# A recurrence and a gated product on one core: v loaded in fp32 by SP and cast by GpSimd, w_in issued together and earlier, some loads held back

## The chip, the cores and the metric

The kernel runs on one core of a Trainium2 chip. The metric is the time of one execution on the device in microseconds (us), less is better. Engines are named as in the profile: PE is TensorE (PEld its weight loads), DVE is VectorE, ACT is ScalarE, POOL is GpSimd, SP is SyncE.

## What is computed

```python
def _attn_ref(q, k, v, f_logit):                 # each (4, 8, 768, 48)
    f = 1.0 / (1.0 + np.exp(-f_logit))
    state = np.zeros((B, H, D, D))
    for t in range(S):
        state = f[:, :, t, :, None] * state + np.einsum('bhd,bhe->bhde', k[:, :, t], v[:, :, t])
        y[:, :, t] = np.einsum('bhd,bhde->bhe', q[:, :, t], state)

def _moe_ref(x, w_in, w_out, a, b):              # x (3072, 384), w_in (384, 2048), w_out (2048, 384)
    h = x @ w_in
    P = a[0] + a[1] * h + a[2] * h * h + a[3] * h * h * h
    Q = 1.0 + np.abs(b[0]) * np.abs(h) + np.abs(b[1]) * h * h
    return (P / (Q + 1e-06)) @ w_out
```

A gated linear recurrence over 768 steps is run for 4 batches of 8 heads of size 48; its output, with the heads side by side, goes through a matrix product, a rational function of each element and a second matrix product. All inputs and the output are fp32.

## The kernel before, in words

The sequence is cut into chunks of 256 steps. A *unit* is one chunk of one batch, so there are 12 units (unit n is chunk n // 4 of batch n % 4). Within a unit the recurrence is done in blocks of 64 steps as matrix products, and the state is handed on from block to block and from chunk to chunk.

The order of all work is written out by hand in the string `ORDER`: each entry is a step with the number of its unit, and each engine and each queue carries out its own steps in the order in which they stand there. The steps of one unit n:

- `ld n f|k|q|v` loads an input. f, k and q come in fp32 by SP's queue; v comes by POOL's queue, which casts it to bf16 on the way (tile `vn`). The tiles of the loads have three buffers each.
- `ef`, `ls` (ACT) make the logarithm of the gate, `cs` (PE) its running sum, `A` (ACT) the exponentials, `xa` (DVE) the products of k (x=1) and q (x=0) with them, `T` (PE) and `Te` (ACT, DVE in unit 0) their transposes.
- `sc` (PE) are the scores of a half of the heads, `mk` (DVE) multiplies them with the causal mask out of PSUM.
- `yi` (PE) is the part of the output from the old state, `yb` (PE) the part from inside the block. `yb` uses v as its weights in pieces of 32 columns, since a head has 48; the piece that lies across two heads comes from the tile `vmp`, which `vm n 0` and `vm n 1` (POOL) fill with 16 columns each.
- `kv` (PE) multiplies k with v into the state, `si` adds the old state, `ae` (ACT) and `st` (DVE) scale it; `ye` (ACT, in part DVE in unit 0) brings the output to SBUF as `xT`.
- `h n m0 m1` (PE) multiplies `xT` with four blocks of `w_in` (`ha`, `hb` do the same in two parts); `hy` copies the result, `sq`, `ab`, `p1`, `p2`, `pm`, `tv`, `gm` (DVE), `u` (PE), `ln`, `lz`, `ex` (ACT) make the rational function, and `zd`, `ta` are additions done by DMAs on POOL's queue.
- `o` (PE) multiplies with `w_out`, `oe` copies, `so` stores.
- `wi m0 m1` and `wo m0 m1` load four blocks of `w_in` and `w_out` by POOL's queue with a cast to bf16; `dz` are products that nobody reads.

A step with `>mark` waits until the step of that name has ended (`behind`); what stands behind it on the same engine or queue waits with it. In the order before, `wi 8 12` stands behind unit 0's first `kv`, `wi 12 16 >ls.1` waits for unit 1's logarithm, and `wi 4 8` and `wi 0 4` follow on POOL's queue among the copies and loads of v.

Of the kernel before, what the change touches and what calls it, by code (L numbers as in the profile page):

```python
# [38 lines left out]
hy 2 8 12; wo 0 4; mk 3 0; cs 4 @0; ls 5; vm 4 0; h 2 12 16 @2; vm 3 0; tv 0 0 8; A 4 0; ld 8 f; ld 5 q; A 4 1
xa 4 0; yi 3 1 @3; ld 6 k; yb 3 0 2; hy 2 4 8; ld 6 q; u 1 4 8 @0; xa 4 1; hy 2 12 16; yb 3 2 4; gm 0 8 16  # L40
cs 5 @1; ld 6 v; ye 3 s; T 4 @2; gm 0 0 8; A 5 0; ln 1 4 8; h 3 0 4 @3; p1 2 0 16; Te 4 s; h 3 12 16 @0
ab 2 0 16; hy 3 0 4; o 0 1 8 12 @2; tv 1 0 8; A 5 1; kv 4 @3; hy 3 12 16; sq 2 0 16; u 1 0 4 @1; ae 4; ex 1 8 16
o 0 0 8 12; si 4 0; o 0 1 12 16; xa 5 1; vm 5 1; ln 1 0 4; h 3 8 12 @0; zd 2 8 16; p2 2 0 16; ld 8 k; ef 6
h 3 4 8 @1; ef 7; pm 2 0 16; hy 3 8 12; o 0 1 4 8; hy 3 4 8; sc 4 1 @0; o 0 1 0 4; ls 6; mk 4 1; ta 2 8 16
sc 4 0 @1; ex 1 0 8; o 0 0 0 4; ld 9 f; xa 5 0; cs 6 @0; mk 4 0; o 0 0 4 8; A 6 1; o 0 0 12 16; st 4 0; A 6 0
yb 4 0 2 @1; ab 3 0 16; yb 4 2 4; oe 0 0 2 s; yi 4 0; yi 4 1; si 4 1; sq 3 0 16; ye 4 s; T 5 @2; ef 8
u 2 0 4 @1; Te 5 s; h 4 4 8 @0; st 4 1; zd 3 8 16; ln 2 0 4; gm 1 8 16; h 4 12 16 @2; lz 2 8 16; p1 3 0 16
sc 5 0 @3; h 4 0 4 @1; xa 6 0; hy 4 4 8; vm 6 1; ta 2 0 8; gm 1 0 8; hy 4 12 16; ld 9 q; h 4 8 12 @0; vm 5 0
ld 7 k; ld 7 v; hy 4 0 4; mk 5 0; vm 6 0; u 2 4 8 @2; zd 3 0 8; hy 4 8 12; pm 3 0 16; o 1 1 4 8 @1; ln 2 4 8
o 1 0 0 4; ex 2 8 16; sc 5 1 @2; kv 5 @0; mk 5 1; yi 5 0 @3; yb 5 0 2; ls 7; o 1 0 12 16; sq 4 0 16; o 1 0 4 8  # L50
# [575 lines left out]
```

## Time and profile before

| | |
|---|---|
| timed runs | 215.76, 216.56, 216.99 us; median 216.56 us |
| profiled execution | span 214.4 us from the first to the last instruction; no other time of its own is given |
| busy us in the span | PE 201.0, DVE 201.7, ACT 195.8, POOL 83.7 |
| granted TensorE clock | 1.000 |
| DMA | 43.20 MB, mean 202 GB/s |
| POOL's DMA queue (q0) | 23.86 MB, 21,520 packets |
| SP's DMA queue (q1) | 18.68 MB, 39,360 packets |

In rows of instructions the first number is the start and the second the duration in us, then engine, line of the kernel, operation, the tile written, the tile read, shape and count; a bracket names the idle time before it and what ended that. In rows of groups the numbers behind the bars are busy us, mean ns of one, and idle us before them.

### The profile page before, as it was taken

The numbers are of one execution on the slowest core, as the hardware profiler recorded it, in microseconds if no ns is written. First come the engines' busy times: TensorE is split into PE (matmuls) and PEld (weight loads), VectorE is DVE, ScalarE is ACT, GpSimd is POOL, SyncE is SP. The second block draws the span as 40 slices with busy tenths as digits, with TensorE's granted clock in tenths as the row PEclk, the third lists the DMA queues.
The fourth block names the chain that finished last, engine by engine and source line by source line (L and its number), as shares of the span: only waits on it lengthen the run. The fifth ranks groups of instructions, "written<-read, shape, count | busy, mean of one in ns | idle before, by whom it ended". The sixth has DMA issues, their size and how long they took to land.

```text
span 214.4 us, 7128 instructions
## 1 busy us (share of the span) xinstructions
PE 201.0 (94%) x3166; PEld 139.9 (65%) x3166; DVE 201.7 (94%) x213; ACT 195.8 (91%) x204; POOL 83.7 (39%) x93
## 2 busy tenths in 40 slices
PE   5875999899999999999999899999999999999993
PEld 1544587567767686586687587686577676776461
DVE  4786899999999999999999999999999999999991
ACT  3574689999999999999999999999999999999990
POOL 5161009009165072183270496696350603114200
PEclk9999999999999999999999999999999999999999
DMA  5999999999999999999999499999499896988823
GB/s 143 240 257 217 201 242 197 195 223 223 187 200 248 247 235 219 253 228 203 192 292 193 81 294 215 209 225 208 89 192 200 164 196 126 174 282 151 187 84 148
DMA packets 61199, 43.20 MB, mean 202 GB/s; under 512 B 51184, under 2 KB 55024, under 8 KB 61168
## 3 DMA queue, kind: packets, MB, share of 16 engines
q0 software_dynamic: 21520, 23.86, 67.3%
q1 hardware_dynamic: 39360, 18.68, 34.5%
q8 instruction: 25, 0.41, 0.8%
q10 hardware_dynamic: 288, 0.20, 0.3%
q14 instruction: 6, 0.05, 0.1%
HBM read 25.17 MB, written 4.72 MB: 139 GB/s over the span
## 4 chain that ended last, share of the span: by engine, by line
PE 39%; DVE 29%; ACT 14%; DMA 9%; issue 6%; SPq 2%; POOL 1%; DVEq 0%
PE hp L454 13%; PE op L567 12%; DVE gall L557 6%; DMA w_in_sb<-in_moe_w_in_dram 6%; DVE gall L545 4%; ACT qi L527 4%; ACT hy L484 4%; DVE z L497 3%; DVE h L489 3%; DVE scm L353 3%; DMA fn<-in_f_logit_dram 3%; PE u L505 3%; DVE gall L531 3%; PE y L367 2%; DVE hy L536 2%
## 5 line engine op out<-in xcount | busy, mean ns | idle before, releaser
L567 PE MATMUL op<-w_out_sb,gall 128*128 128x384 bf16 x384 | 69.2, 326 | 0.4 <-DVE gall L557 0.4
L454 PE MATMUL hp<-xT,w_in_sb 128*128 128x256 bf16 x564 | 66.7, 273 | 2.1 <-DMA w_in_sb<-in_moe_w_in_dram 2.0
L454 PEld LDWEIGHTS <-w_in_sb 128*128 128x128 bf16 x564 | 54.2, 98 | 11.5 <-DMA w_in_sb<-in_moe_w_in_dram 2.5
L567 PEld LDWEIGHTS <-gall 128*128 128x128 bf16 x384 | 36.1, 98 | 23.6 <-DVE gall L557 0.8
L484 ACT CAST hy<-hp 128x1024 bf16<-128x1024 f32 x47 | 48.1, 1076 | 2.3 <-PE hp L478 1.4
L527 ACT ACTIVATE qi<-lq 128x2048 bf16<-128x2048 f32 (+1 forms) x26 | 48.0, 1861 | 0.1
L360 POOL COPY vmp<-vn 128x128 bf16<-128x128 bf16 x24 | 35.2, 1516 | 28.4 <-DMA vn<-in_v_dram 22.7
L549 POOL DMA_DIRECT2D gall<-hy x20 | 20.0, 1068 | 53.9 <-ACT lsp L276 10.6
L523 ACT ACTIVATE lq<-z 128x2048 f32<-128x2048 bf16 (+1 forms) x20 | 36.8, 1874 | 0.0
L353 DVE TENSOR_TENSOR scm<-sc,mask 128x1024 bf16<-128x1024 f32 x24 | 29.0, 1215 | 1.9 <-PE sc L345 1.7
L489 DVE TENSOR_TENSOR h<-hy 128x4096 bf16<-128x4096 bf16 (+2 forms) x19 | 28.5, 1500 | 0.0
L557 DVE TENSOR_TENSOR gall<-gall,qi 128x4096 bf16<-128x4096 bf16 (+2 forms) x17 | 28.2, 1666 | 0.2
L545 DVE TENSOR_TENSOR gall<-gall,h 128x4096 bf16<-128x4096 bf16 (+2 forms) x17 | 28.1, 1652 | 0.0
L519 POOL DMA_DIRECT2D z<-h x17 | 19.3, 1366 | 17.0 <-PE u L505 6.0
L302 ACT ACTIVATE A<-cs 128x768 f32<-128x768 f32 (+1 forms) x26 | 19.4, 799 | 1.8 <-PE cs L286 1.8
L193 POOL DMA_DIRECT2D vn<-in_v_dram x12 | 12.4, 1030 | 15.7 <-PE y L367 7.9
L531 DVE TENSOR_SCALAR gall<-hy,a_sb 128x4096 bf16<-128x4096 bf16 (+1 forms) x14 | 16.9, 1208 | 0.0
L536 DVE TENSOR_SCALAR hy<-hy,a_sb 128x4096 bf16<-128x4096 bf16 (+1 forms) x14 | 16.6, 1185 | 0.0
L497 DVE TENSOR_SCALAR z<-hy 128x4096 uint16<-128x4096 uint16 (+2 forms) x19 | 15.7, 834 | 0.4 <-ACT hy L484 0.4
L330 ACT COPY qkT<-tp 128x1024 f32<-128x1024 f32 x11 | 11.6, 1058 | 3.2 <-PE tp L320 3.2
L320 PE MATMUL tp<-ident,qkp 128*128 128x128 bf16 x192 | 12.9, 219 | 0.8 <-DVE qkp L308 0.5
L320 PEld LDWEIGHTS <-qkp 128*128 128x128 bf16 x192 | 11.5, 98 | 2.5 <-DVE qkp L308 0.9
(73 smaller groups left out, 255.8 us busy)
## 6 DMA issues: line engine op xcount, KB each, us to landing
gall<-hy POOLq DMA_DIRECT2D x18, 512.0 KB, 7.1
z<-h POOLq DMA_DIRECT2D x15, 512.0 KB, 8.4
fn<-in_f_logit_dram SPq DMA_DIRECT2D x11, 384.0 KB, 8.5
kn<-in_k_dram SPq DMA_DIRECT2D x11, 384.0 KB, 12.1
qn<-in_q_dram SPq DMA_DIRECT2D x11, 384.0 KB, 11.3
out_dram<-osb SPq DMA_DIRECT2D x11, 384.0 KB, 5.1
vn<-in_v_dram POOLq DMA_DIRECT2D x12, 192.0 KB, 8.9
w_in_sb<-in_moe_w_in_dram POOLq DMA_DIRECT2D x4, 384.0 KB, 10.1
```

What stands on the lines that cost most here:

```text
L320: nc.tensor.transpose(t[:, x, i, p, :], s["qk"][:, i, x, 2 * p:2 * p + 2, :].rearrange("t h d -> t (h d)"), ident)
L353: return nc.vector.tensor_mul(t, s["sc", g].rearrange("s r a i t -> s (r a) (i t)"), mb)
L360: nc.gpsimd.tensor_copy(s["vm"][:, :, :, 32 * x:32 * x + 16], src)
L454: nc.tensor.matmul(t[:, m - m0, :], w_in_sb[:, kk, m * P:(m + 1) * P], s["x"][:, kk].rearrange("p i j t -> p (i j t)"), start=(kk == 0), s ...
L484: (nc.scalar.copy if eng == "s" else nc.vector.tensor_copy)(fl(big(s, "hy", "hy", 3), m0, m1), fl(s["hp", m0], 0, m1 - m0))
L489: return nc.vector.tensor_mul(fl(big(s, "h2", "h2", 2), m0, m1), fl(s["hy"], m0, m1), fl(s["hy"], m0, m1))
L523: nc.scalar.activation(fl(lq, m0, m1), fl(s["z"], m0, m1), AF.Ln, scale=regs[2], bias=1.0 + 1e-6)
L527: nc.scalar.activation(fl(qi, m0, m1), fl(lq, m0, m1), AF.Exp, scale=-1.0)
L531: return nc.vector.tensor_scalar(fl(big(s, "g", "gall", 3), m0, m1), fl(s["hy"], m0, m1), a_sb[:, 3:4], a_sb[:, 2:3], op0=ALU.mult, op1=AL ...
L545: return nc.vector.tensor_mul(fl(s["g"], m0, m1), fl(s["g"], m0, m1), fl(s["h2"], m0, m1))
L557: return nc.vector.tensor_mul(fl(s["g"], m0, m1), fl(s["g"], m0, m1), fl(qi, m0, m1))
L567: nc.tensor.matmul(s["op", j][:, j, 0:DM], s["g"][:, m, P * j:P * j + P], w_out_sb[:, m, :], start=(s["on", j] == 1), stop=(s["on", j] == KF))
```

## The change

v is loaded in fp32 by SP's queue into a tile with a single buffer. A new step `vc n par` casts the heads of one parity into `vpd`, where each head has 64 columns: even heads lie at columns 0 to 47 and odd ones at 16 to 63, the rest is zero. `yb` and `kv` read their weights and operand from there, and `vm` and `vmp` are gone. `vc` runs on POOL, but for unit 0 (one on ACT, one on DVE) and unit 10 (both on DVE). Many `vc` steps have a mark, and `ld n+1 v` stands behind the second `vc` of unit n. Because SP's queue issues in order, a v load that waits for its buffer holds the loads behind it.

The four loads of `w_in` are issued one after the other behind `ls.0.2.4`, unit 0's second logarithm. `ld 2 k` waits for `xa.1.0`, and `ld 2 q`, `ld 3 f`, `ld 3 k`, `ld 3 q` stand behind it. The mask is bf16. All else stands in the order as before.

The start of the order, before and after:

```
-ld 0 q 0 2; ld 1 f; ld 0 v; ab_ a s; ld 1 k; fa; ld 1 q; ef 0 2 4; ef 0 0 2; cz 3; ls 0 0 2; ls 0 2 4; cz 1
-cs 0 2 4 @2; cs 0 0 2 @3; A 0 0 2 4; dz 4 @0; A 0 1 2 4; xa 0 0 2 4; A 0 1 0 2; xa 0 1 2 4; A 0 0 0 2
-xa 0 1 0 2; T 0 2 4 @0; vm 0 1; kv 0 @3; Te 0 2 4; wi 8 12; xa 0 0 0 2; ae 0; sc 0 1 @0; si 0 0; mk 0 1
-T 0 0 2 @2; ef 1; dz 5 @1; fr; Te 0 0 2; ld 2 f >mk.0.1; ls 1; ld 3 f; st 0 0; sc 0 0 @0; ld 2 k; cs 1 @2
-wi 12 16 >ls.1; mk 0 0; ld 2 q; ld 3 k; yi 0 1 @1; vm 0 0; A 1 1; ld 1 v; ld 3 q; yb 0 2 4; yb 0 0 2; A 1 0
-si 0 1; wi 4 8; ye 0 0 1 v; ye 0 1 3 s; xa 1 1; wi 0 4; h 0 8 12 @1; xa 1 0; ld 2 v; fb; T 1 @0; hy 0 8 12 v
+ld 0 q 0 2; ld 0 v; ld 1 f; ab_ a s; ld 1 k; fa; ld 1 q; ef 0 2 4; ef 0 0 2; cz 3; ls 0 0 2; ls 0 2 4
+wi 8 12 >ls.0.2.4; wi 12 16; wi 4 8; wi 0 4; cz 1; cs 0 2 4 @2; cs 0 0 2 @3; A 0 0 2 4; dz 4 @0; A 0 1 2 4
+xa 0 0 2 4; A 0 1 0 2; xa 0 1 2 4; A 0 0 0 2; xa 0 1 0 2; T 0 2 4 @0; vc 0 0 s; vc 0 1 v; ld 1 v; kv 0 @3
+Te 0 2 4; xa 0 0 0 2; ae 0; sc 0 1 @0; si 0 0; mk 0 1; T 0 0 2 @2; ef 1; dz 5 @1; fr; Te 0 0 2; ld 2 f >mk.0.1
+ls 1; st 0 0; sc 0 0 @0; cs 1 @2; mk 0 0; yi 0 1 @1; A 1 1; yb 0 2 4; yb 0 0 2; A 1 0; si 0 1; ye 0 0 1 v
+ye 0 1 3 s; xa 1 1; h 0 8 12 @1; xa 1 0; ld 2 k >xa.1.0; ld 2 q; ld 3 f; ld 3 k; ld 3 q; fb; T 1 @0; hy 0 8 12 v
```

The steps of v in the rest of the order after: `vc 1 0 >ab.0.8.12`, `vc 1 1 >sq.0.8.12; ld 2 v`; `vc 2 0; vc 2 1; ld 3 v` behind `sc 2 0`; `vc 3 0 >p2.0.0.8`, `vc 3 1 >st.2.0; ld 4 v`; `vc 4 0 >pm.1.0.8`, `vc 4 1 >mk.3.1; ld 5 v`; and so on to `vc 9 0; vc 9 1; ld 10 v`, `vc 10 0 v; vc 10 1 v; ld 11 v`, `vc 11 0 >p1.8.0.16`, `vc 11 1 >p2.8.0.16`.

The code:

```diff
-    mask = consts.tile([P, 2, 2, R], F32, name="mask")
+    mask = consts.tile([P, 2, 2, R], BF16, name="mask")
-    vmp = [consts.tile([P, 2, HP, 48], BF16, name=f"vmp{i}") for i in range(2)]
+    vpd = [consts.tile([P, HP, 2, 2, E], BF16, name=f"vpd{i}") for i in range(2)]
...
-        eng = nc.gpsimd if what == "v" else nc.sync
         if what not in s:
-            s[what] = ld.tile([P, H, 2, D], BF16 if what == "v" else F32, name=what + "n")
+            s[what] = ld.tile([P, H, 2, D], F32, name=what + "n", bufs=1 if what == "v" else 3)
         hh = slice(2 * a0, 2 * a1)
-        i = eng.dma_start(out=s[what][:, hh].rearrange("p h i d -> p h (i d)"),
+        i = nc.sync.dma_start(out=s[what][:, hh].rearrange("p h i d -> p h (i d)"),
...
-            nc.vector.memset(vmp[i][:, :, :, 16:32], 0.0)
+            nc.vector.memset(vpd[i][:, :, 0, :, D:E], 0.0)
+            nc.vector.memset(vpd[i][:, :, 1, :, 0:E - D], 0.0)
...
-    def vm(n, x):
-        vv = s["v"].rearrange("p (a r) i d -> p r i a d", r=2)
-        src = vv[:, 0, :, :, 32:48] if x == 0 else vv[:, 1, :, :, 0:16]
-        nc.gpsimd.tensor_copy(s["vm"][:, :, :, 32 * x:32 * x + 16], src)
+    def vc(n, par, *args):
+        hold = [x[1:] for x in args if x.startswith(">")]
+        copy = nc.scalar.copy if "s" in args else (nc.vector if "v" in args else nc.gpsimd).tensor_copy
+        i = copy(s["vp"][:, :, par, :, 16 * par:16 * par + D],
+                 s["v"].rearrange("p (a r) i d -> p r a i d", r=2)[:, par])
+        if hold:
+            behind(i, hold[0])
...
-                        if kk == 1:
-                            w = s["vm"][r, i0, a, 16 * par:16 * par + 32]
-                        else:
-                            w = s["v"][r, 2 * a + par, i0, 16 * par:16 * par + 32]
+                        e = 32 * (kk - par)
+                        w = s["vp"][r, a, par, i0, e:e + 32]
...
-                                         s["qk"][r, i, 1, 2 * a + par, :], s["v"][r, 2 * a + par, i, :],
+                                         s["qk"][r, i, 1, 2 * a + par, :], s["vp"][r, a, par, i, 16 * par:16 * par + D],
```

More of the change, by code (lines that the diff above doesn't have):

```diff
@@ new lines @@
+hy 8 4 8; dz 2 @2; lz 6 0 8; si 10 0; sc 9 1 @3; T 10 @2; mk 9 1; o 5 0 0 4; ex 6 8 16; sq 8 0 16; yi 9 0 @3
+yi 9 1; yb 9 2 4; o 5 1 4 8; ae 10; Te 10 s; o 5 1 0 4; p2 7 0 16; ex 6 0 8; dz 3 @2; ab 8 0 16; yb 9 0 2
+o 5 1 8 12; ye 9 s; o 5 0 8 12; gm 6 0 16; zd 8 0 8; lz 7 0 8; o 5 0 12 16; ta 7 0 8; o 5 1 12 16; h 9 0 4 @2
+ta 7 8 16; st 10 0; oe 5 0 2 s; p1 8 0 16; zd 8 8 16; ex 7 0 8; sc 10 1 @1; h 9 8 12 @0; mk 10 1
+vc 11 0 >p1.8.0.16; hy 9 0 4; h 9 4 8 @3; xa 11 0; hy 9 8 12; xa 11 1; sc 10 0 @2; hy 9 4 8; yi 10 1 @1
@@ new lines @@
+p2 8 0 16; yi 10 0; h 9 12 16 @0; lz 7 8 16; mk 10 0; vc 11 1 >p2.8.0.16; T 11 @3; pm 8 0 16; hy 9 12 16
+o 6 1 12 16 @2; o 6 0 8 12; Te 11 s; o 6 1 0 4; ex 7 8 16; ab 9 0 16; sc 11 0 @0; ta 8 8 16; yb 10 0 2
+o 6 0 0 4; ta 8 0 8; sq 9 0 16; lz 8 0 8; yb 10 2 4; o 6 0 12 16; o 6 1 8 12; ye 10 s; mk 11 0; o 6 0 4 8
+zd 9 0 8; lz 8 8 16; o 6 1 4 8; zd 9 8 16; gm 7 0 16; h 10 0 4 @0; oe 6 0 2 s; h 10 8 12 @1; hy 10 0 4
+p1 9 0 16; ex 8 8 16; sc 11 1 @2; h 10 12 16 @0; mk 11 1; p2 9 0 16; kv 11 @3; hy 10 8 12; o 7 0 4 8 @2
@@ new lines @@
+hy 11 12 16; o 8 1 4 8; lz 10 0 8; h 11 4 8 @0; gm 9 0 16; ta 10 0 8; o 8 0 0 4; lz 10 8 16; o 8 1 12 16
+h 11 0 4 @2; p1 11 8 16; ex 10 0 8; ab 11 12 16; ab 11 8 12; o 9 0 4 8 @1; sq 11 12 16; zd 11 8 12; o 9 1 4 8
+tv 10 8 16; zd 11 12 16; o 9 0 12 16; ex 10 8 16; o 9 1 12 16; p2 11 8 16; o 9 1 0 4; pm 11 8 12; hy 11 4 8
+o 9 0 0 4; gm 10 0 16; ta 11 8 12; o 9 1 8 12; hy 11 0 4; o 9 0 8 12; oe 8 0 2 s; sq 11 4 8; lz 11 8 12
+o 10 0 8 12 @0; so 8 0 2 s; pm 11 12 16; o 10 1 4 8; lz 11 12 16; ab 11 4 8; ta 11 12 16; o 10 1 12 16
@@ new lines @@
+ab 11 0 4; sq 11 0 4; ex 11 8 12; u 11 4 8 @3; p1 11 0 8; oe 9 0 2 s; o 10 1 8 12; zv 11 0 4; o 10 0 0 4
+ex 11 12 16; gm 11 8 12; so 9 0 2 s; o 10 1 0 4; p2 11 0 8; ln 11 4 8; o 10 0 4 8; pm 11 4 8; o 10 0 12 16
+ex 11 4 8; gm 11 12 16; o 11 1 8 12 @3; pm 11 0 4; lz 11 0 4; o 11 0 8 12 @2; tv 11 4 8; o 11 1 12 16; gm 11 4 8
+ex 11 0 4; o 11 0 12 16; tv 11 0 4; oe 10 0 2 s; o 11 0 4 8; gm 11 0 4; o 11 1 4 8; so 10 0 2 s; o 11 0 0 4
+o 11 1 0 4; oe 11 0 1 v; dz 1 @1; so 11 0 1 s; oe 11 1 2 s; so 11 1 2 a
@@ L174, in unit @@
             c, b = divmod(n, B)
-            units[n] = dict(c=c, b=b, qk=qkp[n % 2], ls=lsp[n % 2], vm=vmp[n % 2], st=states[b])
+            units[n] = dict(c=c, b=b, qk=qkp[n % 2], ls=lsp[n % 2], vp=vpd[n % 2], st=states[b])
         return units[n]
@@ L588 @@
                  cz=const_z, fa=coef_a, fb=coef_b, fr=coef_r, ef=ef, ls=ls, cs=cs, A=A, xa=xa, T=T, Te=Te,
-                 sc=sc, mk=mk, vm=vm, yi=yi, yb=yb, kv=kv, si=si, ye=ye, ae=ae, st=st, h=h, ha=ha, hb=hb, hy=hy, sq=sq, ab=ab, u=u, ln=ln,
+                 sc=sc, mk=mk, vc=vc, yi=yi, yb=yb, kv=kv, si=si, ye=ye, ae=ae, st=st, h=h, ha=ha, hb=hb, hy=hy, sq=sq, ab=ab, u=u, ln=ln,
                  zv=zv, zd=zd, sa=sa, lz=lz, ex=ex, p1=p1, p2=p2, pm=pm, ta=ta, tv=tv, gm=gm, o=o, oe=oe, so=store, dz=dz)
```

124 lines of the change are left out of this document (53 added, 71 removed).

## The prediction

> **What bounds the kernel now.** The page came first, then the busy times by stretch, then the start-up in order of time on each engine, then the DMA view cut into short windows, and last the groups by line and form.
>
> ```profile
> span 214.4 us, 7128 instructions
> PE 201.0 (94%) x3166; PEld 139.9 (65%) x3166; DVE 201.7 (94%) x213; ACT 195.8 (91%) x204; POOL 83.7 (39%) x93
> PE 39%; DVE 29%; ACT 14%; DMA 9%; issue 6%; SPq 2%; POOL 1%; DVEq 0%
> ```
> ```profile
> 10.00:20.00 10.00, 7.31 (x163) 4.93 (x160) 8.57 (x15) 4.75 (x7) 4.67 (x7) 1.00 1.30 242
> 20.00:30.00 10.00, 8.42 (x197) 6.35 (x198) 8.03 (x13) 8.07 (x12) 0.53 (x2) 1.00 1.30 211
> 60.00:100.00 40.00, 40.00 (x653) 28.45 (x651) 40.00 (x34) 40.00 (x45) 19.02 (x16) 1.00 1.17 232
> ```
>
> In the second fence the columns after the length are busy us of PE, PE's weight loads, DVE, ACT and POOL, then the granted clock (1.00), the DMA share and GB/s. From 60 to 100 us PE, DVE and ACT are each busy for all 40 us. A stall or an extra instruction there is paid in full, and nothing can be saved by moving work. Only the start-up has holes: from 10 to 30 us DVE rests for 3.4 us and ACT for 7.2. So the question is how much of the hole in the start-up the change closes or widens, and what it adds to the three full engines. The chain, with 39% on PE, passes from PE to ACT to DVE as these full engines take turns.
>
> The hole, in order of time, with the wait in brackets:
>
> ```profile
> 15.38 0.60 ACT L436 ACTIVATE xT<-y 128x512 bf16<-128x512 f32 x1
> 16.13 0.95 DVE L308 TENSOR_TENSOR qkp<-qn,A 128x768 bf16<-128x768 f32 x1
> 16.81 1.48 PE L454 MATMUL hp<-xT,w_in_sb 128*128 128x256 bf16 x12 [1.74 <-DMA w_in_sb<-in_moe_w_in_dram]
> 18.13 1.06 PE L320 MATMUL tp<-ident,qkp 128*128 128x128 bf16 x16
> 19.22 1.01 ACT L330 COPY qkT<-tp 128x1024 f32<-128x1024 f32 x1 [3.25 <-PE tp L320]
> 21.08 0.61 PE L478 MATMUL hp<-xT,w_in_sb 128*128 128x256 bf16 x4 [1.90 <-DMA w_in_sb<-in_moe_w_in_dram]
> 21.62 0.64 PE L345 MATMUL sc<-qkT 48*64 48x128 bf16 x32
> 22.09 1.23 DVE L353 TENSOR_TENSOR scm<-sc,mask 128x1024 bf16<-128x1024 f32 x1 [1.74 <-PE sc L345]
> 23.24 0.68 DVE L489 TENSOR_TENSOR h<-hy 128x1024 bf16<-128x1024 bf16 x1
> 24.13 0.44 PE L414 MATMUL sv<-vn,qkp 64*64 64x48 bf16 x32 [0.23 <-DMA vn<-in_v_dram]
> 25.29 0.56 DVE L445 TENSOR_TENSOR state<-sv,alast 128x384 bf16<-128x384 f32 x1 [0.23 <-ACT alast L441]
> 31.98 0.69 DVE L497 TENSOR_SCALAR z<-hy 128x2048 uint16<-128x2048 uint16 x1 [0.35 <-ACT hy L484]
> ```
>
> PE takes its work in the written order: unit 0's first w_in product (`h 0 8 12`), unit 1's transposes (`T 1`), the next product (`ha`), unit 1's scores (`sc 1`). Two of the four wait for w_in, and DVE's 1.74 us before the masking of unit 1 (22.09) is what those two waits leave. After 22.09 DVE waits only 0.23 and 0.35 us up to 33 us.
>
> **w_in in one go, and who it meets.** The wait `>ls.0.2.4` lets POOL issue all four loads when unit 0's logarithm ends, at 5.66 + 0.94 = 6.60; they were at 9.63, 12.83 and from 14.72.
>
> ```profile
> 5.66 0.94 ACT L276 ACTIVATE lsp<-fn 128x384 bf16<-128x384 f32 x2
> 9.63 0.76 POOL L199 DMA_DIRECT2D w_in_sb<-in_moe_w_in_dram  x1
> 4.32 0.58 SPq L193 DMA_DIRECT2D fn<-in_f_logit_dram  x1
> 6.34 0.51 SPq L193 DMA_DIRECT2D kn<-in_k_dram  x1
> 6.90 2.47 SPq L193 DMA_DIRECT2D qn<-in_q_dram  x1
> ```
> ```profile
> fn<-in_f_logit_dram SPq DMA_DIRECT2D x1, 384.0 KB, 6.4
> qn<-in_q_dram SPq DMA_DIRECT2D x1, 384.0 KB, 6.8
> q1 hardware_dynamic: 562, 0.21, 113.4%
> q0 software_dynamic: 6, 0.01, 6.1%
> q0 software_dynamic: 175, 0.18, 124.6%
> q0 software_dynamic: 162, 0.14, 85.8%
> q1 hardware_dynamic: 160, 0.06, 36.1%
> ```
>
> The first two rows of the last fence are issues with the us to landing. The others are packets and MB of a queue in a window: SP's queue (q1) alone from 3.6 to 4.3; POOL's (q0) from 11.8 to 12.4; POOL's from 12.94 to 13.8, w_in with SP nearly empty; both from 22 to 23.
>
> Read so: SP alone moves 562 / 0.7 = 803 packets a us. A 384 KB load in packets of 0.21 MB / 562 is 1,024 packets. w_in moves alone at 175 / 0.86 = 203 a us in packets of 1.03 KB, so its four loads are some 1,530. Where both have work (22 to 23) they go packet for packet, 160 each a us. The load issued at 9.63 shows 6 packets by 12.4, so data begin some 2.4 us after the issue, in the changed kernel at 9.0.
>
> What SP still owes then: f of unit 1 landed at 4.32 + 6.4 = 10.7, cleared by about 9.7 if landing trails by 1 us (my estimate), so 560 of its packets are left at 9.0, v of unit 0 having taken the place on SP that it had on POOL. Then k and q of unit 1, 2,048 more. Packet for packet, w_in needs 1,530 / 160 = 9.6 us, to 18.6. SP moves as many, and its last 1,080 take 1.3 us: q is through at 19.9 and lands at 20.9. If w_in went first altogether, it would be 9.0 + 7.5 + 2,608 / 803 + 1 = 20.7, the same. Before, q landed at 6.90 + 6.8 = 13.7 and was used at 16.13. So w_in is bought from k and q of unit 1, and only an SP queue that is served first escapes that.
>
> From q on the chain is fixed: the product with A (0.95), the transposes (1.06), their copy (1.01), 0.2 of hand-overs: the scores at 24.1 instead of 21.62, **+2.5**. f lands at 9.0 + 560 / 160 + 1 = 13.5, 2.7 late, which puts x of unit 0 (15.98 before) at 18.7, ahead of q and so hidden. With SP served first, q lands by 14.3, the first product begins when x is there, at about 16.3, then 1.3 + 1.06 + 1.01 and hand-overs: scores at 19.8, **-1.8**. I take +2.5, since the two rows from 22 to 23 are the ones here with both queues stocked. Holding k, q of unit 2 and unit 3 behind `xa.1.0` frees no time before that step. Every SP load written behind it waits too, but what they feed is written after unit 1's scores, and SP then stands empty: nothing, 0.5 at most if f of unit 3 is late for ACT. The hole of 0.35 at 31.98 goes, as w_in is long there: **-0.35**.
>
> **v through SP, the copies.** kv of unit 1 now reads the padded copy, and POOL's second copy waits for `sq.0.8.12`, which ends at 23.24 + 0.68 = 23.92.
>
> ```profile
> 24.14 0.53 POOL L360 COPY vmp<-vn 128x128 bf16<-128x128 bf16 x2 [7.03 <-DMA vn<-in_v_dram]
> 32.68 1.28 POOL L360 COPY vmp<-vn 128x128 bf16<-128x128 bf16 x1 [8.01 <-DMA vn<-in_v_dram]
> 60.74 4.63 POOL L360 COPY vmp<-vn 128x128 bf16<-128x128 bf16 x1 [2.45 <-DMA vn<-in_v_dram]
> L445 DVE TENSOR_TENSOR state<-sv,alast 128x384 bf16<-128x384 f32 x20 | 10.9, 547 | 0.2 <-ACT alast L441 0.2
> 140.00 1.31 DVE L497 TENSOR_SCALAR z<-hy 128x4096 uint16<-128x4096 uint16 x1
> 103.28 1.21 DVE L497 TENSOR_SCALAR z<-hy 128x4096 uint16<-128x4096 uint16 x1
> ```
>
> No row has a POOL copy of 384 fp32 elements. Free of DVE, one of 128 took 0.27 (two in 0.53), so the new one lies between 0.27 and 0.81; I take 0.55, as part of the 0.27 is fixed. kv of unit 1 then comes 24.5 against 24.13, and the state step at 25.29 waited for it already: **+0.4** (0 to 0.7). Unit 10's two copies go to DVE in its full stretch; the nearest DVE row with 384 elements is the state step, 0.547. A copy from SBUF may run faster, but not at zero: twice 0.45, **+0.9** (0.4 to 1.1). Unit 0's copies on ACT and DVE fall into the start, ahead of a wait for q, and cost nothing while q is late (0.5 if q is early). The bf16 mask, two more memsets before 7 us, and weights read from `vpd` keep the shapes: nothing.
>
> Beside DVE, POOL copies stood 1.28 and 4.63 us, and DVE's z took 1.31 beside one against 1.21 without. 24 copies by 0.1 would be 2.4 saved at most if all interference went. Most new copies are held behind a step that is followed by a masking or state step, which read PSUM; I take **-0.5** (-2.4 to 0).
>
> ```profile
> vn<-in_v_dram POOLq DMA_DIRECT2D x12, 192.0 KB, 8.9
> fn<-in_f_logit_dram SPq DMA_DIRECT2D x11, 384.0 KB, 8.5
> kn<-in_k_dram SPq DMA_DIRECT2D x11, 384.0 KB, 12.1
> 44.85 0.44 PE L414 MATMUL sv<-vn,qkp 64*64 64x48 bf16 x32
> ```
>
> The Trainium skill (SBUF — State Buffer, section "Who interferes with whom") states that DVE and GpSimd take a shared pair of ports for a whole instruction, the first to start blocking the other. The 4.63 us copy agrees for POOL's side; DVE's 0.1 us does not show it for DVE's. The same section would have SP's loads escape what POOL's suffer: by it v should land sooner and the wait of 0.23 at 24.13 would go, +2.7 in place of +2.95. The rows do not show it: v took 8.9 us by POOL, f 8.5 and k 12.1 by SP, so I count nothing.
>
> **The sum:** 2.5 - 0.35 + 0.4 + 0.9 - 0.5 = +2.95 on a span of 214.4. The median of the runs, 216.56, stands 2.16 above that span, taken as constant: 219.5.
>
> **Rivals.** *Faster: SP is served first.* For it: POOL's queue is slow to wake (6 packets 2.8 us after the issue at 9.63), so SP may be through first. Against: 2,048 packets need 2.5 us even alone, and the rows from 22 to 23. It decides if q of unit 1 lands before 18.2, where +2.5 becomes zero. Time: -1.8 - 0.35 + 0.4 + 0.5 + 0.9 - 0.5 = -0.85, and with the low ends of the copies (0, 0, 0.4, -2.4) -4.15: between 215.7 and 212.4, about 215.0. Chance 0.25.
>
> *Slower still: the single v buffer.* v had three buffers and now has one, so v of unit 3 is loaded only after both copies of unit 2, and its own copies must be done before kv of unit 3 (44.85). If v of unit 2 lands near 33 as before (the copy at 32.68 waited for it), two copies take 1.1, the next load 8.5 to 12.1, its copies 1.1: 43.7 to 47.3. A stall holds PE, and ACT soon after; the SP loads ordered between the two make the late half likelier when it happens at all. Price about 2: 221.5. Chance 0.20.
>
> *The port lock to the letter.* The four POOL copies without a hold (units 2 and 9) and those that overrun their masking step block DVE: some 3 us at 0.55 to 0.81 each, 222.5. Chance 0.06.
>
> *Even.* q lands near 18, between the two ends: 216.6. Chance 0.12.
>
> **How the numbers follow.** The forecast has 0.37, with 218.3 to 220.8 as its own range. Slower is 0.37 + 0.20 + 0.06 = 0.63; same 0.12; faster 0.25. The bound is 0.5%, about 1.1 us, which is what a measurement of this kernel can tell from no change. The range runs from 214.6, most of the fast case, to 222.3; some 0.1 lies below it and 0.1 above.
>
> **What would show it.** Right: the queue windows from 9 to 18 us hold w_in and SP packets in like numbers, unit 1's product with q starts near 21, the scores near 24, and DVE rests some 4 us from 15 to 24. Wrong: that product at 16 and scores before 21. The ring of v shows as a wait of PE for POOL's copy at unit 3's kv, near 45; the lock, as DVE instructions 0.3 us or more above their form beside a POOL copy.

## The result, and the profile after

The changed kernel takes 232.41 us (median of four runs, 231.63 to 233.0) where the kernel before took 216.78 beside it: a ratio of 1.0724 (95% interval 1.0683 to 1.0765). That is slower, as forecast, but by 15.6 us where 2.9 were forecast, and outside the range. The profiled execution took 233.0 us with a span of 231.3, against 214.4 before: 16.9 us to find. In some kernels below the timed runs lie in two groups a few us apart; ratios and intervals are those of the faster group, and the profiles of the kernels `e6_warm` and `e8_v_mended` are from the other one.

The page of the changed kernel, its totals, the engines of the chain that ended last, and the granted clock in 40 slices:

```profile
span 231.3 us, 7146 instructions
PE 207.2 (90%) x3158; PEld 143.9 (62%) x3166; DVE 203.4 (88%) x218; ACT 197.0 (85%) x205; POOL 59.5 (26%) x77
PEclk9999569999799999999999999999799999999999
PE 34%; DVE 26%; DMA 23%; issue 8%; SPq 5%; POOL 2%; ACT 1%; DVEq 0%; POOLq 0%
```

DVE and ACT have hardly more work than before (203.4 for 201.7, 197.0 for 195.8), so the time went into waiting: DMA's share of the chain rose from 9% to 23%. PE has 6.2 us more of busy time with no more matmuls, and the clock has three dips that the kernel before did not have: some matmuls ran slower. Each dip follows a wait of PE, one at each of the three places below.

Where the time went is read best from one repeated step. PE's product of k with v (`kv`) starts for each unit at these times, in us:

| | kv 1 | kv 2 | kv 4 | kv 10 | kv 11 | span |
|---|---|---|---|---|---|---|
| before | 24.13 | 38.27 | 61.68 | 145.78 | 174.62 | 214.4 |
| changed | 31.94 | 46.79 | 75.16 | 159.22 | 191.30 | 231.3 |
| lag | 7.8 | 8.5 | 13.5 | 13.4 | 16.7 | 16.9 |

From unit 4 to unit 10 nothing is lost. There are three places: the start (8.5), units 2 to 4 (5.0) and units 10 to 11 (3.3).

**The start.** In order of time on DVE and PE of the changed kernel:

```profile
20.33 0.96 DVE L309 TENSOR_TENSOR qkp<-kn,A 128x768 bf16<-128x768 f32 x1 [4.27 <-DMA kn<-in_k_dram]
23.75 0.96 DVE L309 TENSOR_TENSOR qkp<-qn,A 128x768 bf16<-128x768 f32 x1 [2.45 <-DMA qn<-in_q_dram]
24.76 1.03 PE L321 MATMUL tp<-ident,qkp 128*128 128x128 bf16 x8 [2.79 <-DVE qkp L309]
27.84 1.07 PE L346 MATMUL sc<-qkT 48*64 48x128 bf16 x32
28.84 1.89 PE L479 MATMUL hp<-xT,w_in_sb 128*128 128x256 bf16 x8
```

Unit 1's products with k and q, at 15.26 and 16.13 before, now wait for their loads. The packets and MB of the queues in windows of the changed kernel, SP's queue (q1) in 8 to 9 us, then both in 11 to 12, then both in 14 to 18:

```profile
q1 hardware_dynamic: 684, 0.26, 127.1%
q0 software_dynamic: 171, 0.18, 109.9%
q1 hardware_dynamic: 6, 0.00, 0.3%
q0 software_dynamic: 590, 0.59, 86.5%
q1 hardware_dynamic: 588, 0.22, 32.1%
```

From 14 to 18 us the two queues go packet for packet (590 and 588), and as w_in's packets are larger it takes 0.59 of the 0.81 MB. From 11 to 12 us SP got 6 packets. So q of unit 1 landed at 23.65.

What then came is in the busy times of stretches of the changed kernel (columns as in the prediction; the granted clock is the third number from the right):

```profile
20.00:24.00 4.00, 0.62 (x8) 0.45 (x8) 1.21 (x2) 0.00 (x0) 0.00 (x0) 0.89 1.20 266
24.00:28.00 4.00, 2.14 (x20) 1.44 (x24) 3.22 (x7) 2.13 (x3) 0.50 (x1) 0.50 0.73 164
28.00:32.00 4.00, 4.00 (x48) 2.38 (x48) 2.96 (x3) 1.48 (x2) 0.51 (x1) 0.50 1.17 266
```

After PE had worked 0.62 us in four, its clock stood at half until 32 us. The `hb` product at 28.84 took 1.89 us, before 1.05.

**Units 2 to 4.** The chain of the changed kernel in order of time (start, us, what), from unit 1's last step to the stall:

```profile
30.73 1.29 PE cs L287 x4
33.22 7.33 DMA vn<-in_v_dram
40.67 1.96 POOL vpd L360 x2
42.65 9.96 DMA vn<-in_v_dram
52.76 0.02 POOL vpd L360
52.78 2.41 issue
55.18 1.50 POOL vpd L360
56.73 0.43 PE sv L415 x31
```

This is the single v buffer: load, copies, load, copies, one after the other, until PE has all of unit 3's `kv` from 56.73 on. The two copies of unit 3 stood from 52.76 to 56.68. PE waited for each of them, and behind the wait its clock was low. PE of the changed kernel, its stretch from 56 to 60 us, and the same transposes before:

```profile
55.29 0.18 PE L415 MATMUL sv<-vpd,qkp 64*64 64x48 bf16 x1 [2.13 <-POOL vpd L360]
56.73 0.43 PE L415 MATMUL sv<-vpd,qkp 64*64 64x48 bf16 x31 [1.26 <-POOL vpd L360]
57.32 1.87 PE L321 MATMUL tp<-ident,qkp 128*128 128x128 bf16 x16
56.00:60.00 4.00, 3.27 (x60) 2.88 (x60) 0.78 (x2) 1.69 (x3) 2.32 (x3) 0.65 0.52 124
45.44 1.05 PE L320 MATMUL tp<-ident,qkp 128*128 128x128 bf16 x16
```

So the 5.0 us are 3.4 of waiting and 1.6 of slower matmuls: from 56.73 to `kv 4` it took 18.4 us, before, from 44.85, 16.8.

**Units 10 and 11.** Rows of SP, POOL and DVE of the changed kernel, and the issue of q with its us to landing:

```profile
136.79 2.90 SPq L581 DMA_DIRECT2D out_dram<-osb  x3
137.97 1.72 POOL L520 DMA_DIRECT2D z<-h  x2 [2.85 <-issue]
139.79 1.58 SPq L193 DMA_DIRECT2D kn<-in_k_dram  x1
141.42 3.31 SPq L193 DMA_DIRECT2D qn<-in_q_dram  x1
144.83 11.55 SPq L193 DMA_DIRECT2D vn<-in_v_dram  x2
154.07 0.96 DVE L309 TENSOR_TENSOR qkp<-qn,A 128x768 bf16<-128x768 f32 x1 [1.53 <-DMA qn<-in_q_dram]
155.35 0.63 DVE L360 CAST vpd<-vn 128x384 bf16<-128x384 f32 x2 [0.33 <-DMA vn<-in_v_dram]
161.77 0.81 PE L568 MATMUL op<-w_out_sb,gall 128*128 128x384 bf16 x4 [1.82 <-DVE scm L354]
qn<-in_q_dram SPq DMA_DIRECT2D x1, 384.0 KB, 12.6
```

PE then waits 1.82 us for DVE, and the clock falls once more. The same transposes in the changed kernel and before, and the stretch of the changed kernel:

```profile
163.68 1.89 PE L321 MATMUL tp<-ident,qkp 128*128 128x128 bf16 x16
148.05 1.07 PE L320 MATMUL tp<-ident,qkp 128*128 128x128 bf16 x16
164.00:166.00 2.00, 2.00 (x18) 1.66 (x17) 2.00 (x2) 0.65 (x2) 0.00 (x0) 0.50 0.81 160
```

The kernel before issued the same q, behind the same stores, and it landed in 5.9 us, long before its use. There POOL was still at its v copies and came to the additions (`zd`) only at 129.97, behind those stores and loads:

```profile
121.45 6.40 POOL L360 COPY vmp<-vn 128x128 bf16<-128x128 bf16 x3 [0.49 <-issue]
129.97 2.07 POOL L519 DMA_DIRECT2D z<-h  x2
```

In the changed kernel POOL is free, issues them at 137.97 among the stores, and k and q share the DMA engines with their 1 MB (two of 512 KB). That these additions are what slows q is read from the order of the rows; no run moved them.

### The profile page after: what moved, and what is told of

Read it like the earlier page. It is cut to its first block, busy times and chain, and to the rows that moved or that the text cites. A ratio compares the mean times of both kernels' runs of the same rounds, so it can differ in the third digit from the quotient of the medians.

```text
span 231.3 us, 7146 instructions
## 1 busy us (share of the span) xinstructions
PE 207.2 (90%) x3158; PEld 143.9 (62%) x3166; DVE 203.4 (88%) x218; ACT 197.0 (85%) x205; POOL 59.5 (26%) x77
## 4 chain that ended last, share of the span: by engine, by line
PE 34%; DVE 26%; DMA 23%; issue 8%; SPq 5%; POOL 2%; ACT 1%; DVEq 0%; POOLq 0%
DMA vn<-in_v_dram 12%; PE op L568 12%; PE hp L455 8%; DMA qn<-in_q_dram 7%; DVE gall L558 6%; SPq L193 4%; DMA gall<-hy 4%; DVE gall L546 4%; PE tp L321 3%; DVE scm L354 3%; DVE gall L532 3%; DVE z L498 2%; DVE qkp L309 2%; PE y L370 2%; PE u L506 2%
## 5 line engine op out<-in xcount | busy, mean ns | idle before, releaser
L455 PE MATMUL hp<-xT,w_in_sb 128*128 128x256 bf16 x564 | 67.5, 274 | 1.0 <-ACT xT L437 1.0
L528 ACT ACTIVATE qi<-lq 128x2048 bf16<-128x2048 f32 (+1 forms) x26 | 47.3, 1836 | 0.1
L520 POOL DMA_DIRECT2D z<-h x17 | 18.2, 1139 | 53.2 <-DVE h L490 18.3
L550 POOL DMA_DIRECT2D gall<-hy x20 | 19.0, 1033 | 46.9 <-PE cs L287 14.4
L360 POOL CAST vpd<-vn 128x384 bf16<-128x384 f32 x20 | 17.0, 861 | 54.2 <-DVE z L498 17.1
L321 PE MATMUL tp<-ident,qkp 128*128 128x128 bf16 x192 | 15.3, 238 | 7.2 <-DVE qkp L309 6.9
L321 PEld LDWEIGHTS <-qkp 128*128 128x128 bf16 x192 | 13.2, 107 | 9.6 <-DVE qkp L309 8.0
L532 DVE TENSOR_SCALAR gall<-hy,a_sb 128x4096 bf16<-128x4096 bf16 (+1 forms) x14 | 16.8, 1201 | 0.0
L537 DVE TENSOR_SCALAR hy<-hy,a_sb 128x4096 bf16<-128x4096 bf16 (+1 forms) x14 | 16.8, 1202 | 0.0
L446 DVE TENSOR_TENSOR state<-sv,alast 128x384 bf16<-128x384 f32 x20 | 11.1, 553 | 6.5 <-PE sv L426 4.5
L498 DVE TENSOR_SCALAR z<-hy 128x4096 uint16<-128x4096 uint16 (+2 forms) x19 | 16.1, 858 | 0.0
```

What stands on the lines that cost most here:

```text
L321: nc.tensor.transpose(t[:, x, i, p, :], s["qk"][:, i, x, 2 * p:2 * p + 2, :].rearrange("t h d -> t (h d)"), ident)
L455: nc.tensor.matmul(t[:, m - m0, :], w_in_sb[:, kk, m * P:(m + 1) * P], s["x"][:, kk].rearrange("p i j t -> p (i j t)"), start=(kk == 0), s ...
L498: return nc.vector.tensor_scalar(fl(big(s, "z", "z", 2), m0, m1).bitcast(U16), fl(s["hy"], m0, m1).bitcast(U16), 0x7FFF, None, op0=ALU.bit ...
L528: nc.scalar.activation(fl(qi, m0, m1), fl(lq, m0, m1), AF.Exp, scale=-1.0)
L532: return nc.vector.tensor_scalar(fl(big(s, "g", "gall", 3), m0, m1), fl(s["hy"], m0, m1), a_sb[:, 3:4], a_sb[:, 2:3], op0=ALU.mult, op1=AL ...
```

## The experiments

**The parts of the start.** Theory 1: the three places above, each with its own cause. Theory 2: v on SP's queue is the whole cost and w_in is innocent.

`e1_win_hold`, the kernel before with w_in in one go and the held loads, v as before:

```
- kv 0 @3; Te 0 2 4; wi 8 12; ... wi 12 16 >ls.1; ... wi 4 8; ... wi 0 4
+ ls 0 0 2; ls 0 2 4; wi 8 12 >ls.0.2.4; wi 12 16; wi 4 8; wi 0 4; cz 1
- ls 1; ld 3 f; ... ld 2 k; ... ld 2 q; ld 3 k; ... ld 3 q
+ xa 1 0; ld 2 k >xa.1.0; ld 2 q; ld 3 f; ld 3 k; ld 3 q
```

> The kernel before with only the second half of the change: the four loads of w_in in one go behind ls.0.2.4, and k, q of unit 2 and unit 3 held behind xa.1.0; v as before. Theory 1 (the change costs in three places: w_in meets k and q of unit 1 at the start, about +8 us; v's single buffer at units 2 and 3, about +5; q and v of unit 10, about +3): unit 1's scores late by 3 to 5 us against 21.6 and the kernel slower by 4 to 7 us, some 221 to 224, since v of units 0 and 1 are not ahead on SP's queue here. Theory 2 (v on SP's queue is the whole cost, w_in is innocent): within 1.5 us of the kernel before.

Measured: 221.41 us (220.47 to 221.66) against 216.52, ratio 1.0225 (1.0198 to 1.0253). Theory 2 falls: 5 us come without any change to v.

```profile
21.77 0.96 DVE L309 TENSOR_TENSOR qkp<-qn,A 128x768 bf16<-128x768 f32 x1 [5.34 <-DMA qn<-in_q_dram]
```

That wait on DVE puts unit 1's scores at 25.44 for 21.62; `kv 2` is 5.5 late and so is the end.

`e2_v_only`, the changed kernel with w_in and the held loads back at their places:

```
- ls 0 2 4; wi 8 12 >ls.0.2.4; wi 12 16; wi 4 8; wi 0 4; cz 1
+ xa 0 1 0 2; wi 8 12 >xa.0.1.0.2; ... wi 12 16 >ls.1; mk 0 0; wi 4 8 >mk.0.0; wi 0 4
- xa 1 0; ld 2 k >xa.1.0; ld 2 q; ld 3 f; ld 3 k; ld 3 q
+ ls 1; ld 3 f; ... ld 2 k; ... wi 0 4; ld 2 q; ld 3 k; ld 3 q
```

> The changed kernel with w_in and the loads of units 2 and 3 at the places that they had before, so only v differs from the kernel before. Theory 1: the start costs 1 to 2 us at unit 1's scores, units 2 to 3 cost 5 and unit 10 costs 3: some 225 to 227. Theory 2: the same loss as the whole change, 230 to 233.

Measured: ratio 1.0521 (1.0476 to 1.0566); runs from 226.87 to 233.03, the profile with a span of 226.7. Its `kv 2` is 3.5 late, `kv 4` 8.7, `kv 11` 12.1: the second and third place are there without the early w_in, and the first has shrunk, not gone.

`e3_win_late`, the changed kernel with all of w_in later, the holds kept:

```
- ls 0 2 4; wi 8 12 >ls.0.2.4; wi 12 16; wi 4 8; wi 0 4; cz 1
+ ls 1; wi 8 12 >ls.1; wi 12 16; wi 4 8; wi 0 4; st 0 0
```

> The changed kernel with one difference: the four loads of w_in wait for unit 1's logarithm (ls.1, about 12.8) in place of unit 0's (6.9). Theory 1: q of unit 1 lands near 14 in place of 23.7, unit 1's scores at 21.5 to 23.5 in place of 27.8, and 5 to 7 us of the whole come back: 225 to 227. Theory 2: q of unit 1 lands late all the same, behind v and f on its queue, and less than 2 us come back: above 230.

Measured: ratio 1.0609 (1.0556 to 1.0662), runs from 228.56 to 236.6. One wait took the place of another: PE waits 4.2 us for w_in itself, and `kv 2` is 3.9 late. The width of the runs leaves the size open.

`x_win_only` has the first two lines of the diff of `e1_win_hold`, `x_hold_only` the last two, each on the kernel before:

> The kernel before with w_in's four loads in one go behind unit 0's logarithm, v as before and nothing held back. Theory 1 (w_in's packets alone set back k and q of unit 1): unit 1's q product near 21.8 us as in the run with the holds (21.77), scores near 25.4, end +5 or more: 220 to 222 us. Theory 2 (much of those 5 us is the held loads of units 2 and 3, which come late for unit 2): scores near 25.4 again, but unit 2 no further behind than unit 1, 218.5 to 220 us.

> The kernel before with only the holds: k and q of unit 2 and f, k, q of unit 3 issued behind unit 1's q product, w_in at its old places. Theory 1: nothing, 216 to 217 us (the prediction held them at nothing, 0.5 at most). Theory 2: k of unit 2 is wanted at about 31 us in the kernel before; issued near 17 with a landing of 10 us or more it may come late by 1 to 2: 217.5 to 218.5 us. A third outcome, faster by 0.5 to 1 because w_in's last quarter lands earlier, would be 215 to 216.

Measured: 221.2 us, ratio 1.0212 (1.0168 to 1.0255), and 220.6 us, 1.0187 (1.0136 to 1.0237), both against 216.51. The first shows w_in alone to be enough (q again at 21.79). The second is above all that was expected. Its chain and ACT:

```profile
18.69 12.67 DMA fn<-in_f_logit_dram
31.39 0.84 ACT L271 ACTIVATE fn<-fn 128x768 f32<-128x768 f32 x1 [5.41 <-DMA fn<-in_f_logit_dram]
```

It was not k of unit 2 but f of unit 3, held behind k and q, and with it ACT, which works in order. The scores of unit 1 were 1.1 us earlier (20.56) before that. The two parts cost 4.7 and 4.1 alone and 4.9 together: work that the early w_in has made late no longer waits for a load that is less late.

On the kernel before, `x_hold_kq` (k and q of units 2 and 3 held, f of unit 3 left; first two lines), `x_win_quarter` (one of w_in's four loads early; last two) and `x_hold_kq_quarter` (both):

```
- ld 2 k; ... ld 2 q; ld 3 k; ... ld 3 q
+ xa 1 0; ld 2 k >xa.1.0; ld 2 q; ld 3 k; ld 3 q; ld 2 v
- Te 0 2 4; wi 8 12; xa 0 0 0 2
+ ls 0 2 4; wi 8 12 >ls.0.2.4; cz 1; ... Te 0 2 4; xa 0 0 0 2
```

> The kernel before with k and q of units 2 and 3 held behind unit 1's q product, f of unit 3 left at its old place. Theory 1 (in the run with all the holds unit 1 was 1.1 us earlier, because w_in no longer shares its time with k of unit 2, and the whole loss came after it from f of unit 3, for which ScalarE waited 5.41 us at 31.4): unit 1's scores again near 20.6 to 21.0, no wait for f, 215.2 to 216 us, faster than before by 0.2 to 0.6 %. Rival (k and q of unit 2, issued at 17.5 and landing 10 to 12 us later, are late as well, wanted at 30.7 and 34.2 in the kernel before): 217 us or more.

> The kernel before with one of the four loads of w_in, the first to be used, issued behind unit 0's logarithm (near 7 instead of 9.6), the other three at their old places: a dose of the early w_in. By packet-for-packet sharing 384 packets in front of k and q of unit 1 set q back by a quarter of what four do (5.2 us of wait plus the 2.4 that q lay ready before its use in the kernel before: 7.6), so by 1.9, less than those 2.4: no wait for q, the wait of TensorE for w_in at 16.81 (1.74 us) shorter: 215.5 to 216.5 us. If instead any early w_in blocks q: 218 to 219 us.

> Both of the edits above: k and q of units 2 and 3 held behind unit 1's q product, f of unit 3 at its old place, one quarter of w_in early. If the two gains add: 214.6 to 215.6 us, which would beat both kernels; if they come out of the same wait for w_in: as the better of the two.

Measured, twelve runs each: 216.81 us, ratio 1.0003 (0.9974 to 1.0032); 215.07 us, 0.9946 (0.9914 to 0.9978); 215.23 us, 0.9936 (0.9908 to 0.9965). The hold of k and q alone gains nothing, against what was expected: PE waited 2.09 us for w_in at 17.51, where without f of unit 3 in `x_hold_only` it had been 1.12 at 16.55. Behind that wait the clock was 0.51 from 18 to 20 us, and unit 1's scores came at 23.11. The quarter is faster than both kernels, by 0.5%; with the hold added it gains no more. DVE and PE of `x_win_quarter`:

```profile
17.30 0.96 DVE L309 TENSOR_TENSOR qkp<-qn,A 128x768 bf16<-128x768 f32 x1 [0.59 <-DMA qn<-in_q_dram]
16.52 1.47 PE L455 MATMUL hp<-xT,w_in_sb 128*128 128x256 bf16 x12 [0.96 <-ACT xT L437]
```

PE no longer waits 1.74 us for w_in, and q is just late. The dose was mis-sized: one quarter set q back from 13.7 to 17.2, by 3.5 and not 1.9. All four quarters set it back by 8.

**The ring.** `e4_spare` gives unit 2's v a second buffer, in the part of `w_out`'s tile that is idle then, and lets unit 3's load go:

```diff
+            if what == "v" and n == 2:
+                s[what] = w_out_sb[:, 0:4, :].rearrange(...).bitcast(F32).rearrange(...)
- ld 2 v; kv 1 @3; ... vc 2 0; vc 2 1; ld 3 v; kv 2 @1
+ ld 2 v; ld 3 v; kv 1 @3; ... vc 2 0; vc 2 1; kv 2 @1
```

> The changed kernel with one difference: v of unit 2 goes into the part of w_out's tile that is loaded last, so it has a buffer of its own, and v of unit 3 is issued right behind it, before the copies of unit 2. Theory 1: kv of unit 3 no longer waits for its copies (3.4 us of PE idle and the gap of 10 us between unit 2's and unit 3's kv shrinks to about 6.5), and 4 to 5 us come back: 227 to 229. Rival (the copies themselves, slow beside DVE, are the cost at that place, not the load behind them): less than 1.5 us come back.

Measured: 226.13 us (225.96 to 226.75), ratio 1.0457 (1.0434 to 1.0479): 6.3 back, more than expected. `kv 4` starts at 68.88 instead of 75.16, and PE has no wait for POOL's copy left in units 2 to 4. Of the 6.3, 1.0 is there at `kv 2` already (45.76 for 46.79), where the clock was back at 1.00 from 32 us on instead of 0.83. Unit 3's copies took 0.51 each, at the steps for which they are held, so this run takes away the late load and the slow copies together.

**Unit 10.** `e5_q10` is the changed kernel with q of unit 10 ahead of the stores:

```
- lz 5 8 16; so 3 0 2 s; so 2 0 2 s; so 1 0 2 s; ... ld 11 k; ld 10 q
+ lz 5 8 16; ld 10 q; so 3 0 2 s; so 2 0 2 s; so 1 0 2 s; ... ld 11 k
```

> The changed kernel with unit 10's q issued ahead of the output stores of 136.8 us instead of behind them and k of unit 11. Theory 1 (q of unit 10, issued at 141.4 and landed at 154, starts the 3.3 us that units 10 and 11 lose): 2 to 3 of them come back, 229.5 to 231 us. Rival (v of unit 10, issued only at 144.8 behind unit 9's copies and landed at 155.3, holds the unit anyway, and q is merely the first to be seen): at most 0.5 back, 232 to 233 us.

Measured: 229.89 us (229.55 to 230.78), 2.5 back. From `kv 10` to `kv 11` it takes 29.52 us (32.08 in the changed kernel, 28.84 before). PE's wait of 1.82 is 0.35 and the transposes take 1.07 again, so wait and slow clock went together. What stays, 0.7, is the size of the two copies on DVE (0.63).

`e9_spare_q10` has both diffs, of `e4_spare` and of `e5_q10`:

> The changed kernel with both mends that lie behind the start: the second fp32 buffer for unit 2's v and unit 10's q ahead of the output stores. If the two places are independent, their gains add (6.3 and 2.5 off 232.4): 223 to 224.5 us, and what is left over the kernel before (about 7) is the start alone. If the second is fed by the first (the collision at unit 10 exists only because all runs late): 225.5 to 226.5 us, no better than the buffer alone.

Measured: 225.06 us (224.46 to 225.44), ratio 1.0398 (1.0356 to 1.0441), between the two expectations. Its span is 1.5 shorter than with the buffer alone, so the gains add in part. What is over the kernel before, 8.4 us, is there at `kv 2` already (7.5 late).

**What v costs with all three mended.** `e8_v_mended` has the diffs of `e2_v_only`, `e4_spare` and `e5_q10`; `e10_v2_early` besides this one:

```
- ld 2 q; ld 3 k; ld 3 q; ... vc 1 1 >sq.0.8.12; ld 2 v; ld 3 v
+ ld 2 q; ld 2 v; ld 3 k; ld 3 q; ... vc 1 1 >sq.0.8.12; ld 3 v
```

> The changed kernel's fp32 v by SP's queue and its casts, with w_in and the loads of units 2 and 3 at the places of the kernel before, a second fp32 buffer for unit 2's v (idle space of w_out's tile), and q of unit 10 early. Theory 1 (start, single buffer and unit 10 are all there is): what is left is 0.7 to 3.5 from the longer v on SP's queue and the casts in units 0 to 2: 217.5 to 220.5 us. Rival (v in fp32 and its casts cost all along: 20 casts of 0.86 us beside VectorE's work, twice the bytes): 223 to 226 us.

> The kernel with all three places mended, and besides v of unit 2 loaded into the second buffer ahead of k and q of unit 3 instead of behind seven loads. Theory (what was left, 3.4 us in its better runs and more in the others, is v of unit 2: in its profile it was issued at 31.7, landed at 42.6 and TensorE waited 3.71 us for the cast): no wait for that cast, unit 2's product with v near 39.5 to 40, 216.5 to 218.5 us. Rival (the casts and the longer v cost beside VectorE and on the queue wherever they stand): 219.5 us or more.

Measured: ratio 1.0157 (1.0104 to 1.0209), with runs from 219.67 to 223.74; and 219.91 us (219.73 to 220.16), 1.0155 (1.0115 to 1.0196). Moving v of unit 2 took its wait away and the spread with it, but the ratio stayed, so that expectation fell. Chain and POOL of `e10_v2_early`:

```profile
12.57 10.93 DMA fn<-in_f_logit_dram
56.13 5.61 POOL L363 CAST vpd<-vn 128x384 bf16<-128x384 f32 x1
```

The first row is what is left: f of unit 2, behind v of unit 1 on SP's queue, lands at 23.50, and ACT waits 2.76 us for it. `kv 1` is 1.9 late, `kv 2` 3.0 (the clock was 0.74 from 28 to 32 us), `kv 11` 3.6. The time is one that the rival had named (219.5 or more), but not for its reason: from `kv 2` to `kv 11`, where most of the casts stand, only 0.6 is added, and a copy of 5.61 us beside DVE did no harm where it had time. So most of the 3.3 us comes from the start, and by the rows from the longer v on SP's queue; no run tried that by itself.

**The clock.** `e6_warm` puts 26 products that nobody reads into the changed kernel:

```
- h 0 8 12 @1; xa 1 0; ld 2 k >xa.1.0; ... T 1 @0
+ h 0 8 12 @1; dz 26 @2; xa 1 0; ld 2 k >xa.1.0; ... T 1 @0
```

> The changed kernel with 26 more idle matmuls of 512 columns put into TensorE's rest between unit 0's first w_in product and unit 1's transposes (about 18 to 24 us). Theory (part of the loss at the start is the granted clock, which fell to 0.65 in the mean of 20 to 30 us after that rest): hb 1.05 instead of 1.82, cs 0.8 instead of 1.3, unit 1's product with v 1.0 to 2.0 earlier than 31.94, 230.5 to 231.5 us. Rival (the clock follows something else, or the extra matmuls stand in the way of the transposes): clock still down at 26 to 32 us, 232 to 233.5 us.

Measured: ratio 1.0824 (1.0761 to 1.0887), runs from 232.84 to 238.06: no gain. Its stretches:

```profile
24.00:28.00 4.00, 2.10 (x21) 1.33 (x20) 1.56 (x5) 0.00 (x0) 0.00 (x0) 1.00 0.58 148
28.00:32.00 4.00, 2.90 (x50) 1.97 (x49) 3.81 (x6) 3.31 (x4) 0.51 (x2) 1.00 1.01 232
```

The clock stayed at 1.00 from 16 to 36 us, though DVE again waited for q (3.18 us). From the scores to the first product of `kv 1` it took 2.20 us instead of 4.10: the dip costs 1.9 there. The other 31 products then waited for POOL's second copy:

```profile
32.55 0.43 PE L415 MATMUL sv<-vpd,qkp 64*64 64x48 bf16 x31 [0.51 <-POOL vpd L360]
```

In the changed kernel PE came to `kv 1` too late to meet that copy. q's product came 2.6 us later in this profile (26.37 for 23.75), for a reason that no run shows, so `kv 1` was hardly earlier for all that. `kv 2` was 0.5 earlier and `kv 4`, at 75.23, no longer: the single buffer took that back. From `kv 10` to `kv 11` it took 36.28 in this profile, with a wait of 4.05 for v of unit 10; why that load came later than in the changed kernel stays open.

## Why the prediction was right and wrong

The direction and the first mechanism were right: w_in is bought from k and q of unit 1, packet for packet. The size failed at six steps.

- **Landing of q, 20.9; measured 23.65.** Data of w_in were put at 9.0; q0 moved 36 packets from 10 to 11 and 171 from 11 to 12, two us later. The rate was put at 160 each a us from two rows at 22 us; it was 147. 1,530 / 147 = 10.4 from 11.0 gives 21.4 for w_in, and q 2.2 after it. SP's own rate was put at 803 a us; it was 684 from 8 to 9 us and 813 from 22 to 23. The late start spared f of unit 1, so x of unit 0 was ready at 16.70 and not at 18.7; that stood hidden behind q in any case.
- **From q to the scores, 3.2; measured 4.1.** The chain was taken at full clock, where it holds: `e6_warm` took 3.26 (from 26.37 to 29.63). At half clock the transposes took 1.03 for 0.62, and the first part of the next product 1.01 for 0.60. That 3.2 fits is partly luck: it counts 16 transposes where 8 were left to do after q (0.44 too much), and leaves out that part of the product, which PE does ahead of the scores (0.53). With q this gives the scores at 27.84, **+6.2 for +2.5**, and 1.6 more by `kv 1`.
- **The single buffer.** The place (PE waits for POOL's copy at unit 3's `kv`) was right, and it had a chance of 0.20 and a price of 2. It took 5.0, and 6.3 came back. The term that failed is the copies. From the landing of unit 2's v the rival counted 10.7 to 14.3 us: two copies 1.1, a load 8.5 to 12.1, two copies 1.1. It took 16.1: the load, at 9.96, lay in its range, the copies took 1.96 and 3.92. They were priced free of DVE, though the prediction shows smaller copies of 1.28 and 4.63 beside it. v of unit 2 also landed later than the rival's 33, at 40.55, since `ld 2 v` stands behind `vc 1 1`, which waits for unit 1. But PE was as late itself: it was through with the work before unit 3's `kv` at 53.15, 8.3 later than `kv 3` stood before. With 1.1 for each pair of copies the chain would have ended near 53.0 (my estimate from these rows), and PE would hardly have waited; no run tried faster copies alone.
- **Units 10 and 11: nothing foreseen, 3.3.** By the rows the freed POOL issues the additions earlier into the same DMA engines; shown is that q's late landing costs 2.5 of it. The prediction asked what each added load meets, not what the emptied engine sets off.
- **The holds, "nothing, 0.5 at most".** True behind the early w_in (221.41 with, 221.2 without), false by themselves (4.1): the named risk, f of unit 3, was sized at 0.5 and is 5.41.
- **The clock, taken as 1.00 throughout.** Behind the wait at each of the three places it fell to about half. PE's busy time grew by 6.2 us with no more matmuls (1.6 of it between unit 3's `kv` and `kv 4`), more than a third of the 16.9.

Of the small terms, the POOL copy was right (0.55 forecast, 0.50 to 0.51 free of DVE), and so was ACT's and DVE's copy at the start being hidden. Groups by form, POOL, then DVE:

```profile
L360 POOL CAST vpd<-vn 128x384 bf16<-128x384 f32 x20 | 17.0, 861 | 54.2 <-DVE z L498 17.1 <-DVE gall L532 10.1 <-PE hp L455 8.5
L360 DVE CAST vpd<-vn 128x384 bf16<-128x384 f32 x3 | 1.0, 358 | 0.7 <-DMA vn<-in_v_dram 0.7
```

The +0.4 at `kv 1` was not paid, because PE was late: the held copy ended at 30.93, and PE came to `kv 1` only at 31.94. In `e6_warm` and `e3_win_late`, where PE came sooner, it waited 0.51 there. Unit 10's two copies took 0.63 for 0.9. The -0.5 for less interference did not come: the large forms on DVE stand as before (the 128x4096 squares 2,285 ns for 2,281). The lock to the letter is not there either: POOL's copies stretch to 0.86 in the mean and 3.9 for a pair, and of DVE's forms only a few grew (two of 128x2048, 1,361 ns for 1,214).

The account in medians: buffer and unit 10 give back 232.4 - 225.1 = 7.3; w_in in one go with the holds costs 4.9; v on SP's queue with everything mended 3.3. Together 15.5 of 15.6 us; as the parts were measured on different kernels, this is a check and no proof.

## What to carry to other kernels

When a load is moved up, write down who is on the DMA engines then and what each lands for; a quarter of w_in early paid 0.5%, all four cost 2.1%. A buffer count cut to one makes load and use a chain, and its copies are to be priced as they run beside the other engines (3.92 us for a pair here, not 1.1). A wait of PE is to be priced with the slower clock behind it (6.2 us more of PE's busy time here). And of an engine that is freed, ask what it will issue earlier.

## What was not expected of the hardware

The clock: a PE that rested 3.13 and 2.79 us with 0.62 us of work between was granted 0.50 for the next 8 us, though work was there from 26.9. The Trainium skill (TensorE: Matmul & The Clock Gate, section "What's actually happening") says that an idle window of about 3.4 us halves the clock. That idleness halves it agrees: the run with 26 idle products was at 1.00 from 16 to 36 us. The length does not: a rest of 1.82 us (unit 10) was followed by 0.50, and one of 2.09 us (`x_hold_kq`) by 0.51, while rests of 1.74 and 1.90 us in the kernel before left it at 1.00. So the length of one rest did not decide it, and what did is not shown.

The sharing of the DMA engines: the Trainium skill (DMA: Bandwidth & Descriptors, section "Queues, rings and completion order") has them take turns between queues packet by packet. From 14 to 18 us the trace agrees, 590 to 588. From 11 to 12 us it does not, 171 to 6, and no run here shows why.
